# A sparse attention and gated feed-forward kernel: the order of its first loads

## The chip, the cores and the metric

The kernel runs on one core of a Trainium2 chip. The time is the device time of one execution in microseconds (us), and runs are compared by the median. A core has five engines with an instruction stream each: TensorE (PE, matmuls and transposes; PEld are its weight loads), VectorE (DVE), ScalarE (ACT), GpSimd (POOL) and SyncE (SP). Each engine takes its instructions strictly in the order of the program. Transfers are issued by SP, ACT and POOL and carried out by 16 DMA engines that all of them share.

## The reference

```python
# q, k, v: [4 batches, 8 heads, 768 tokens, 64], float32; sampled_blocks: [24, 3]
scores = (q @ k^T) / 8                       # per head, 768 x 768
mask: 24 x 24 blocks of 32 tokens; a block is kept if |i-j| <= 1, if i or j is 0 or 23,
      or if j is one of the three sampled blocks of row i
attn = softmax(where(mask, scores, -1e9)); x = attn @ v      # [4, 768, 512]
h    = relu(x @ w_in)                        # w_in [512, 1024]
conv = sum over k of conv_w[k] * h[token + k - 1]            # 3 taps along the tokens
out  = (h * sigmoid(conv)) @ w_out           # w_out [1024, 512], out [4, 768, 512] float32
```

## The kernel before, in words

**The attention.** The 32 heads are worked on as 16 pairs, P = 0 to 15, four pairs to a batch. A pair's q, k and v are two heads each. q and k of a pair come as bf16 into one of three `nat` buffers, v into one of three `vn` buffers; the load itself converts from float32. PE transposes q and k (`pe_head`, L482), and DVE copies the result out of PSUM (L488) into one of six slots, `ET` (even tokens of the regrouped order) and `OT` (odd ones). Rows 64 to 87 of a slot hold the mask: 24 further rows of the contraction that add a large negative number to the scores of blocks that are left out. The mask rows are the same for all slots. They are built in slot 0 and copied to slots 1 to 5: slot 1 by DVE (`rows_by`, L398, seen in the trace as L371), slots 2 to 5 by transfers that SP issues (`rows_to`, L392), two per slot.

The scores are worked off in 144 *units* of eight 128 x 128 blocks, 18 units to a half n of a batch (n = 0 to 7) and 4.5 units to a pair within it. A unit is: S, the score matmuls (L612) into one of two `st` buffers; the exponential on ACT (L619) of 128 x 1024 elements into one of five `pt` buffers; and AV, eight matmuls with `pt` as weights and v as the moving operand (L639), in two groups of four. v needs a DVE copy from `vn` to `VT` (L468) first. After a pair, DVE divides by the sums (L567, L568), and SP issues a transposing transfer (L589) that lays the pair's output into `xT`.

**The feed-forward.** For each half, when all four parts of `xT` have landed: eight times four matmuls with `winb` (L663), a relu on ACT or DVE (L674, L676), three taps of the convolution on DVE (L687, L693) with edge copies on POOL (L766, L767), the gate as a tanh on ACT (L703) with two DVE steps (L706, L715), then matmuls with `woutb` (L730), an eviction (L739, L741) and the store.

**The order of the work.** The order of each engine's instructions is not written by hand. A list scheduler (`Scheduler.run`) simulates all engines while the program is built. Every operation has durations for the engines that may take it, what it depends on, the buffers that it needs, a latency, an earliest time and a due time (`prio`). The planner repeatedly takes the operation that can start first on its engine and, among those that could start at the same time, the one with the earliest due time. The transfers are simulated as one more engine, `DQ`. The chip then runs each engine's list in that order, whatever the real durations are. `T(u)` is the planned time of unit u; `OFF` is how long after `T(18(n+1))` the feed-forward of half n is due; `S_FIRST`, `A_FIRST`, `R_FIRST` and `N_FIRST` move the due times of S, AV, the relus and the division; `XLAT` and `TLAT` are the planned latencies of the transposing transfers.

**The loads.** `swdge` (L432) issues a load from POOL; it has a `gate`, an operation that has to come first. `qk_loads` issues q and k of a pair, `v_load` its v. q0 and k0 are not among them: they come as float32 by SP and ACT and are converted by DVE or ACT into a `nat` buffer. The four weight loads (two halves of `winb`, two of `woutb`, 512 KB each in bf16, against 192 KB for a q, k or v) have due times 3.3, 3.4, 5.35 and 5.85 there, q of pair P has P, k has P + 0.1 (k1 has 0.6), v has P + 0.2 (v0 has 0.95). In the trace POOL issues in this order: q1, k1, v0, v1, q2, v2, k2, winb first half, q3, v3, k3, winb second half, woutb both halves, q4, k4 and so on.

Of the kernel before, what the change touches and what calls it, by code (L numbers as in the profile page):

```python
# [164 lines left out]
def kernel(  # L165
# [21 lines left out]
    NSLOT = 6  # L187
# [138 lines left out]
    def ind(base, sign, src):  # L326
# [64 lines left out]
    def rows_to(dst, src):  # L391
        return lambda e: nc.sync.dma_start(out=dst[64:88], in_=src[64:88])  # L392
# [4 lines left out]
    def rows_by(dst, src):  # L397
        return lambda e: copy_to(e, dst[64:88], src[64:88])  # L398
    e_mask = {0: op({"DVE": 0.38, "ACT": 0.72}, dup(ET[0]), T(1), [qm_e, km_e], earliest=T0 - 0.5)}
    o_mask = {0: op({"DVE": 0.38, "ACT": 0.72}, dup(OT[0]), T(1), [qm_o, km_o], earliest=T0 - 0.5)}  # L400
    for s in range(1, NSLOT):
        for t, m in ((ET, e_mask), (OT, o_mask)):
            if s == 1:
                m[s] = op({"DVE": 0.58}, rows_by(t[s], t[0]), T(4.5) - 1.5, [m[0]])
            else:
                m[s] = op({"SP": 0.46}, rows_to(t[s], t[0]), T(4.5 * s) - 6, [m[0]], lat=6.0)
    v_one = {}
    for s in range(NSLOT):
        v_one[s] = op({"DVE": 0.06}, lambda e, s=s: nc.vector.memset(VT[s][:, :, :, 64:65], 1.0), -5 + s)
# [22 lines left out]
    def swdge(dst, src, prio, dur, deps=(), early=0.0, alloc=None, uses=(), gate=i_sel,  # L432
              lat=None):
        i_ = op({"POOL": 0.8}, lambda e: nc.gpsimd.dma_start(out=dst(), in_=src), prio,
                list(deps) + [gate], lat=0.6, alloc=alloc, uses=uses, earliest=early)
        return i_, op({"DQ": dur}, None, prio, [i_], lat=lat, uses=(([alloc] if alloc else []) + list(uses)))

    win_ld, wout_ld = [], []
    for x in range(2):
        win_ld.append(swdge(lambda x=x: winb[:, :, 512 * x:512 * x + 512],  # L440
                            moe_w_in.rearrange("(fc p) ff -> p fc ff", p=128)[:, :, 512 * x:512 * x + 512],
                            3.3 + 0.1 * x, 3.0)[1])
        wout_ld.append(swdge(lambda x=x: woutb[:, 4 * x:4 * x + 4, :],
                             moe_w_out.rearrange("(ffc p) o -> p ffc o", p=128)[:, 4 * x:4 * x + 4, :],
                             5.35 + 0.5 * x, 3.0)[1])

    def qk_loads(P):
        b, h0 = P // 4, 2 * (P % 4)
        nb = Buf(P_nat)
        early, late = (T(load_u[P]), 6.0) if P > 3 else (0.0, None)  # L450
        iq, lq = swdge(lambda: dst_of(q, nat_t[nb.index][:, 0], True), src_of(q, b, slice(h0, h0 + 2)), P, 1.25,
                       early=early, alloc=nb, gate=bn1 if P == 1 else i_sel, lat=late)
        if P == 1:
            bn2.deps.append(iq)
        lk = swdge(lambda: nat_t[nb.index][:, 1], src_of(k, b, slice(h0, h0 + 2)), P + 0.1 if P > 1 else 0.6, 1.1, [iq],
                   early=early + (3 if P > 3 else 0), uses=[nb], gate=bn2 if P == 1 else i_sel, lat=late)[1]
        lk.deps.append(lq)
        return nb, lq, lk

    def v_load(P, deps):  # L460
        s = P % NSLOT
        vb = Buf(P_vn)
        b, h0 = P // 4, 2 * (P % 4)
        ld = swdge(lambda: vn_t[vb.index], src_of(v, b, slice(h0, h0 + 2)), P + 0.2 if P else 0.95, 1.1,
                   early=T(load_u[P]) + 6 if P > 3 else 0.0, alloc=vb, lat=6.0 if P > 3 else None)[1]

        def cp(e):
            nc.vector.tensor_copy(out=VT[s][:, :, :, 0:64],  # L468
                                  in_=vn_t[vb.index].rearrange("p h (c d) -> p h c d", c=6))
        return op({"DVE": 0.27}, cp, T(first_u[P]) - (1 if P == 0 else 6), [ld] + deps, uses=[vb, slot_b[P]])  # L470
# [28 lines left out]
    for P in range(NP):  # L499
        s = P % NSLOT  # L500
        if P < min(NPE, NSLOT):

            op({"DVE": 0.0}, None, -100 + P, alloc=slot_b[P])
        if P == 0:
            nb = Buf(P_nat)
            casts = []
            for hh in range(2):
                for x in range(2):
                    def cast(e, hh=hh, x=x, nb=nb):
                        copy_to(e, nat_t[nb.index][:, x, hh], stage0[2 * hh + x])  # L510
                    casts.append(op({"DVE": 0.28, "ACT": 0.4}, cast, -16 + 8 * hh, [hw[2 * hh + x]],
                                    alloc=nb if not casts else None, uses=[] if not casts else [nb]))
            for hh in range(2):
                ce, co = pe_head(0, hh, nb, casts[2 * hh:2 * hh + 2])
                qk_ready[(0, hh)] = [ce, co] + ([qm_e, qm_o, km_e, km_o] if hh == 0 else [e_mask[0], o_mask[0]])
        elif P < NPE:
            nb, lq, lk = qk_loads(P)
            for hh in range(2):
                ce, co = pe_head(P, hh, nb, [lq, lk] + ([slot_first[P]] if P >= NSLOT and hh else [])
                                 + ([slot_first[P - 1]] if P > NSLOT and not hh else []))  # L520
                qk_ready[(P, hh)] = [ce, co, e_mask[s], o_mask[s]]
        else:
            nb, lq, lk = qk_loads(P)
            due = T(first_u[P]) - 10
# [12 lines left out]
            ce = op({"DVE": 0.5}, put(ET, 0), due, [t0, t1, slot_first.get(P - 1)], alloc=slot_b[P], uses=[tb])  # L537
            co = op({"DVE": 0.5}, put(OT, 64), due, [ce], uses=[slot_b[P], tb])
            slot_first[P] = ce
            for hh in range(2):  # L540
                qk_ready[(P, hh)] = [ce, co, e_mask[s], o_mask[s]]
        v_ready[P] = v_load(P, [v_one[s]] + ([slot_first[P]] if P in slot_first else []))


    blk_order = [[(0, 0, 0), (0, 1, 2), (1, 0, 1)], [(1, 1, 0), (1, 2, 2), (0, 2, 1)]]
# [314 lines left out]
```

## Time and profile before

| | |
|---|---|
| runs shown | 229.33, 227.44, 228.6 us: median 228.6 |
| the profiled execution's own time | 229.36 us |
| its span, first to last instruction | 227.6 us |
| mean granted TensorE clock | 0.985 |
| busy in the span: PE, ACT, DVE, POOL | 90%, 84%, 81%, 34% |
| instructions | 6634 |
| DMA | 25.44 MB in all; 11.14 MB through POOL's queue, 13.49 MB through SP's |

Engine rows with a time and a duration are read as "start, duration, engine, line, operation, output <- input, count"; several instructions of a kind in a row are merged into one row. What stands in brackets is the idle time of the engine just before, and what ended it. A row of a table of stretches gives the stretch, its length, then for PE, PEld, DVE, ACT and POOL the busy time and in parentheses the number of instructions, then the granted clock of TensorE, the busy share of the DMA engines and their GB/s. Rows of waits read "who waited, line <- for whom: us in all, times, longest".

### The profile page before, as it was taken

The page shows a single profiled execution, that of the slowest core. Times are in us where ns is not written, and L with a number is a line of the kernel's source. Part 1 is how long each engine was busy: PE and PEld are TensorE (multiplying, and loading weights), DVE is VectorE, ACT ScalarE, POOL GpSimd, SP SyncE. Part 2 cuts the span into 40 slices and gives each one's busy share as a digit, 9 for nine tenths or more (in the row PEclk, how much of TensorE's full clock was granted, in tenths as well). Part 3 has the DMA queues.
Part 4 walks back from the last instruction along what each step waited for, and adds up shares of the span by engine and source line. Part 5 has one row for each costly group of instructions (what it writes and reads, how often), then busy time and mean ns, then how long its engine had stood idle before and what let it go on. Part 6 is the DMA issues. An engine that isn't in the chain of part 4 may idle for free. (4 is left out here: it accounts for less than half of the span.)

```text
span 227.6 us, 6634 instructions
## 1 busy us (share of the span) xinstructions
PE 204.7 (90%) x2592; PEld 153.6 (67%) x2610; DVE 185.3 (81%) x521; ACT 191.1 (84%) x248; POOL 77.8 (34%) x172
## 2 busy tenths in 40 slices
PE   7991699999998998998999999999999999899871
PEld 5881587788776775786778776887776778555330
DVE  5972331169999999999998999899999969999961
ACT  4883299999899989998999998999999999855441
POOL 8771420026364541352634451142132002146000
PEclk9999589999999999999999999999999999999999
DMA  7999999117989499698699856821200230111223
GB/s 170 150 216 205 205 193 167 30 21 93 114 107 122 54 134 208 132 170 115 95 174 138 177 108 145 123 61 57 68 20 20 66 109 20 63 49 46 92 92 138
DMA packets 48838, 25.44 MB, mean 112 GB/s; under 512 B 34768, under 2 KB 45544, under 8 KB 48808
## 3 DMA queue, kind: packets, MB, share of 16 engines
q0 software_dynamic: 18464, 11.14, 39.0%
q1 hardware_dynamic: 30056, 13.49, 26.3%
q8 instruction: 20, 0.33, 0.6%
q10 hardware_dynamic: 288, 0.39, 0.6%
q14 instruction: 10, 0.08, 0.1%
HBM read 23.08 MB, written 6.29 MB: 129 GB/s over the span
## 5 line engine op out<-in xcount | busy, mean ns | idle before, releaser
L619 ACT ACTIVATE pt<-st 128x1024 bf16<-128x1024 f32 x144 | 141.8, 1044 | 12.8 <-PE st L612 12.2
L639 PE MATMUL av<-vt,pt 128*128 128x65 bf16 x1152 | 59.3, 194 | 1.3 <-ACT pt L619 1.2
L687 DVE TENSOR_SCALAR m<-hE,cw 128x384 bf16<-128x384 bf16 x192 | 57.1, 346 | 1.7 <-POOL hE L772 0.7
L639 PEld LDWEIGHTS <-pt 128*128 128x128 bf16 x1152 | 51.0, 98 | 4.1 <-ACT pt L619 2.3
L663 PE MATMUL mix<-xT,winb 128*128 128x384 bf16 x240 | 47.2, 326 | 0.8 <-ACT hE L674 0.4
L766 POOL COPY hE<-hE 128x254 bf16<-128x254 bf16 x32 | 16.8, 524 | 80.0 <-ACT hE L674 38.0
L612 PE MATMUL st<-et,ot 88*128 88x128 bf16 (+1 forms) x224 | 43.0, 236 | 0.7 <-ACT pt L619 0.5
L612 PE MATMUL st<-ot 88*128 88x128 bf16 (+1 forms) x224 | 42.8, 235 | 0.4
L612 PE MATMUL st<-et 88*128 88x128 bf16 (+1 forms) x208 | 42.1, 243 | 0.4
L612 PE MATMUL st<-ot,et 88*128 88x128 bf16 (+1 forms) x208 | 41.6, 241 | 0.9 <-DVE ot L488 0.4
L730 PE MATMUL mix<-woutb,gT 128*128 128x512 bf16 x142 | 39.5, 379 | 3.2 <-DVE hE L676 1.3
L612 PEld LDWEIGHTS <-ot 88*128 88x128 bf16 x448 | 34.7, 98 | 11.1 <-issue 3.0
L612 PEld LDWEIGHTS <-et 88*128 88x128 bf16 x416 | 33.1, 98 | 10.1 <-issue 2.5
L693 DVE TENSOR_TENSOR m<-m 128x768 bf16<-128x768 bf16 x64 | 35.9, 565 | 0.5
L703 ACT ACTIVATE tn<-m 128x768 bf16<-128x768 bf16 x32 | 27.5, 858 | 6.1 <-DVE m L693 5.9
L663 PEld LDWEIGHTS <-winb 128*128 128x128 bf16 x256 | 22.3, 97 | 12.7 <-issue 1.1
L730 PEld LDWEIGHTS <-gT 128*128 128x128 bf16 x192 | 15.8, 97 | 19.0 <-DVE gT L715 3.5
L674 ACT ACTIVATE hE<-mix 128x384 bf16<-128x384 f32 x35 | 17.7, 515 | 2.7 <-PE mix L663 2.6
L568 DVE TENSOR_TENSOR xtok<-av,rcp 128x384 bf16<-128x384 f32 x32 | 17.8, 557 | 1.1
L676 DVE TENSOR_SCALAR hE<-mix 128x384 bf16<-128x384 f32 x25 | 13.8, 550 | 5.0 <-PE mix L663 5.0
L715 DVE TENSOR_TENSOR gT<-tn,hE 128x768 bf16<-128x768 bf16 x32 | 17.6, 549 | 0.1
L567 DVE RECIPROCAL rcp<-av 128x6 f32<-128x6 f32 x32 | 6.0, 189 | 14.0 <-PE av L639 13.9
(75 smaller groups left out, 183.9 us busy)
## 6 DMA issues: line engine op xcount, KB each, us to landing
out_dram<-o2s SPq DMA_DIRECT2D x24, 256.0 KB
vn<-in_v_dram POOLq DMA_DIRECT2D x16, 192.0 KB, 5.1
nat<-in_q_dram POOLq DMA_DIRECT2D x15, 192.0 KB, 4.5
nat<-in_k_dram POOLq DMA_DIRECT2D x15, 192.0 KB, 5.2
winb<-in_moe_w_in_dram POOLq DMA_DIRECT2D x2, 512.0 KB, 13.6
woutb<-in_moe_w_out_dram POOLq DMA_DIRECT2D x2, 512.0 KB, 16.6
xT<-xtok SPq DMA_TRANSPOSE x31
o2s<-in_k_dram ACTq DMA_DIRECT2D x2, 192.0 KB
```

Of the source, the lines that this page charges most:

```text
L568: nc.vector.tensor_tensor(out=xtok_t[xk.index].rearrange("p c h d -> p h c d"), in0=o[:, :, :, 0:64], in1=rcp.unsqueeze(3).broadcast_to([1 ...
L612: nc.tensor.matmul(out=st_t[stb.index][:, 128 * x:128 * (x + n_)], lhsT=QK[kc % 2][s][0:88, 1, hh, kc // 2, :], rhs=QK[par][s][0:88, 0, hh ...
L619: e_op = op({"ACT": t_act(1024)}, lambda e, stb=stb, ptb=ptb: nc.scalar.activation(out=pt_t[ptb.index], in_=st_t[stb.index], func=AF.Exp, ...
L639: nc.tensor.matmul(out=av_t[av_buf[(n, P % 4)].index][:, off:off + 65], lhsT=pt_t[ptb.index][:, 128 * x:128 * x + 128], rhs=VT[P % NSLOT][ ...
L663: nc.tensor.matmul(out=tiles[hb.index][:, 0:384], lhsT=winb[:, fc, 128 * ffc:128 * ffc + 128], rhs=xT_t[xt_buf[n].index][:, fc, :], start= ...
L674: nc.scalar.activation(out=dst, in_=src, func=AF.Relu, bias=0.0, scale=0.5)
L687: nc.vector.tensor_scalar(out=m_t[cb.index][:, slot, o0:o1], in0=src, scalar1=w, scalar2=None, op0=ALU.mult)
L693: nc.vector.tensor_tensor(out=m[:, 0], in0=m[:, 0], in1=m[:, 1], op=ALU.add)
L703: th = op({"ACT": 0.745}, lambda e: nc.scalar.activation(out=tn_t[cb.index], in_=m_t[cb.index][:, 0], func=AF.Tanh, bias=0.0, scale=0.5), ...
L715: nc.vector.tensor_tensor(out=o, in0=t, in1=h, op=ALU.mult)
L730: nc.tensor.matmul(out=acc(), lhsT=gT_t[gb.index][:, ffc, 128 * c:128 * c + 128], rhs=woutb[:, ffc, :], start=(ffc == 0), stop=(ffc == NFF ...
L766: nc.gpsimd.tensor_copy(out=h[:, f0:f0 + 2, 1:128], in_=h[:, f0:f0 + 2, 384:511])
```

## The change

The order of the loads is gated. k of every pair comes right behind its q, and v0 behind k1, v1 behind k2, v2 and v3 behind k3. The weights are issued behind v3. Pair 0's `nat` buffer is taken ahead of all others, so that q3 reuses the buffer of pair 0 and not that of pair 1. The identity matrix (`i_sel`) is made before k1 is issued. The mask rows of slot 2 are copied by DVE too, and the mask transfers of slots 4 and 5 get an earliest planned time of `T(26)` and `T(28)`. The planner's latency of a POOL load changes from 0.6 and 1.9 to 0 and 2.4 us, and the times and offsets for due times have other values.

```diff
-FLEX = 0.0
+FLEX = 0
...
-    T0, PACE0, PACE1 = 8.0, 0.966, 1.0
-    OFF = 14.635
-    XLAT, TLAT = 6.0, 7.0
-    S_FIRST, A_FIRST, R_FIRST, N_FIRST = 1.742, -0.618, 1.2, -0.122
-    F1S, F2A, F2S = 0.062, 1.8, 0.4
+    T0, PACE0, PACE1 = 8.0, 0.9, 1.018
+    OFF = 18.559
+    XLAT, TLAT = 6.652, 8.257
+    S_FIRST, A_FIRST, R_FIRST, N_FIRST = 4.551, -4, 0.593, 1.725
+    F1S, F2A, F2S = 0.03, 1.8, 0.4
...
     i_sel = op({"POOL": 0.3}, ...
-        pattern=[[-1, 128]], channel_multiplier=1), 0.9, [i_mem, bn2])
+        pattern=[[-1, 128]], channel_multiplier=1), -19.2, [i_mem, bn2])
...
-            if s == 1:
-                m[s] = op({"DVE": 0.58}, rows_by(t[s], t[0]), T(4.5) - 1.5, [m[0]])
+            if s < 3:
+                m[s] = op({"DVE": 0.58}, rows_by(t[s], t[0]), T(4.5 * s) - 2.5, [m[0]],
+                            earliest=T(4.5 * s - 4.5))
             else:
-                m[s] = op({"SP": 0.46}, rows_to(t[s], t[0]), T(4.5 * s) - 6, [m[0]], lat=6.0)
+                m[s] = op({"SP": 0.46}, rows_to(t[s], t[0]), T(4.5 * s) - 6, [m[0]], lat=6.0, earliest=T(18 + 2 * s) if s > 3 else 0.0)
...
     i_ = op({"POOL": 0.8}, lambda e: nc.gpsimd.dma_start(out=dst(), in_=src), prio,
-                list(deps) + [gate], lat=0.6, ...)
-        return i_, op({"DQ": dur}, None, prio, [i_], lat=lat, ...)
+                list(deps) + [gate], lat=0.0, ...)
+        return i_, op({"DQ": dur}, None, prio, [i_], lat=lat or 2.4, ...)
...
     (qk_loads)
-        lk = swdge(..., src_of(k, ...), P + 0.1 if P > 1 else 0.6, 1.1, [iq],
-                   early=early + (3 if P > 3 else 0), uses=[nb], gate=bn2 if P == 1 else i_sel, lat=late)[1]
-        lk.deps.append(lq)
+        ik, lk = swdge(..., src_of(k, ...), P + 0.1 if P > 1 else 0.6, 1.1, [iq],
+                   early=early + (3 if P > 3 else 0), uses=[nb], lat=late)
+        k_iss[P] = ik
...
     (v_load)
-        ld = swdge(..., src_of(v, ...), P + 0.2 if P else 0.95, 1.1, ...)[1]
+        v_iss[P], ld = swdge(..., src_of(v, ...), P + 1.15 if P < 3 else P + 0.2, 1.1, ...
+                              gate=k_iss[max(P, min(P + 1, 3))])
...
         if P == 0:
             nb = Buf(P_nat)
+            op({"POOL": 0.0}, None, -100, alloc=nb)
...
     (the weight loads, moved behind all v loads in the text of the program)
-   win_ld:  due 3.3 + 0.1 * x,  DQ 3.0        wout_ld: due 5.35 + 0.5 * x, DQ 3.0
+   win_ld:  due 3.3 + 0.1 * x,  DQ 2.7, gate=v_iss[3]
+   wout_ld: due 3.5 + 0.1 * x,  DQ 2.7, gate=v_iss[3]
```

More of the change, by code (lines that the diff above doesn't have):

```diff
@@ L434, in swdge @@
         i_ = op({"POOL": 0.8}, lambda e: nc.gpsimd.dma_start(out=dst(), in_=src), prio,
[L435 to L445, printed above, removed]
+                list(deps) + [gate], lat=0.0, alloc=alloc, uses=uses, earliest=early)
+        return i_, op({"DQ": dur}, None, prio, [i_], lat=lat or 2.4, uses=(([alloc] if alloc else []) + list(uses)))
+    win_ld, wout_ld, k_iss, v_iss = [], [], {}, {}
     def qk_loads(P):
@@ L541 @@
                 qk_ready[(P, hh)] = [ce, co, e_mask[s], o_mask[s]]
+    for P in range(NP):
+        s = P % NSLOT
         v_ready[P] = v_load(P, [v_one[s]] + ([slot_first[P]] if P in slot_first else []))
+    for x in range(2):
+        win_ld.append(swdge(lambda x=x: winb[:, :, 512 * x:512 * x + 512],
+                            moe_w_in.rearrange("(fc p) ff -> p fc ff", p=128)[:, :, 512 * x:512 * x + 512],
+                            3.3 + 0.1 * x, 2.7, gate=v_iss[3])[1])
+        wout_ld.append(swdge(lambda x=x: woutb[:, 4 * x:4 * x + 4, :],
+                             moe_w_out.rearrange("(ffc p) o -> p ffc o", p=128)[:, 4 * x:4 * x + 4, :],
+                             3.5 + 0.1 * x, 2.7, gate=v_iss[3])[1])
     blk_order = [[(0, 0, 0), (0, 1, 2), (1, 0, 1)], [(1, 1, 0), (1, 2, 2), (0, 2, 1)]]
```

8 lines of the change are left out of this document (4 added, 4 removed).

## The prediction

> **What bounds the kernel now.** I read the slices of the page first, to find out where the engines rest.
>
> ```profile
> PE   7991699999998998998999999999999999899871
> ACT  4883299999899989998999998999999999855441
> PEclk9999589999999999999999999999999999999999
> DMA  7999999117989499698699856821200230111223
> ```
>
> A slice is 5.7 us. From the sixth slice on PE and ACT are full up to the tail. The one hole is in the fourth and fifth slices (17 to 28 us): PE falls to 1, ACT to 3 and 2, the granted clock to 5, and the DMA engines are full. The table of stretches puts numbers to it.
>
> ```profile
> 20.00:30.00 10.00, 5.45 (x59) 4.90 (x60) 3.21 (x7) 2.48 (x3) 3.64 (x5) 0.66 1.27 202
> 30.00:45.00 15.00, 13.83 (x235) 11.90 (x233) 2.30 (x7) 14.86 (x17) 1.41 (x2) 1.00 0.92 127
> 60.00:195.20 135.20, 130.17 (x1764) 100.10 (x1777) 128.23 (x359) 130.35 (x168) 45.95 (x107) 1.00 0.65 104
> 195.20:227.60 32.40, 24.80 (x140) 11.74 (x138) 24.93 (x72) 16.02 (x28) 7.96 (x21) 1.00 0.21 82
> ```
>
> Between 60 and 195 us PE, DVE and ACT are busy for 130.2, 128.2 and 130.4 of 135.2 us. Three engines at 95 to 96% leave some 5 us each to be won, however the work is ordered. So the hole is the place. The chain of waits over the first 40 us, then the rows of PE, DVE and ACT around it:
>
> ```profile
> ACT pt L619 <- PE st L612: 9.9, 7, 7.5
> ```
> ```profile
> 14.80 0.34 PE L482 MATMUL mix<-ident,nat 128*128 128x128 bf16 x3 [0.40 <-DMA nat<-in_k_dram]
> 14.98 0.41 PE L639 MATMUL av<-vt,pt 128*128 128x65 bf16 x8
> ...
> 16.69 0.41 PE L639 MATMUL av<-vt,pt 128*128 128x65 bf16 x8
> ...
> 17.44 0.41 PE L639 MATMUL av<-vt,pt 128*128 128x65 bf16 x8
> 22.19 0.34 PE L482 MATMUL mix<-ident,nat 128*128 128x128 bf16 x3 [4.35 <-DMA nat<-in_q_dram]
> 24.89 0.50 PE L482 MATMUL mix<-ident,nat 128*128 128x128 bf16 x3 [2.36 <-DMA nat<-in_k_dram]
> 25.18 0.42 PE L612 MATMUL st<-et 88*128 88x256 bf16 x1
> ```
> ```profile
> 17.89 0.56 DVE L488 COPY ot<-mix 64x768 bf16<-64x768 bf16 x1
> ```
> ```profile
> 11.24 1.02 ACT L619 ACTIVATE pt<-st 128x1024 bf16<-128x1024 f32 x1 [0.27 <-PE st L612]
> 12.56 2.90 ACT L619 ACTIVATE pt<-st 128x1024 bf16<-128x1024 f32 x3 [0.30 <-PE st L612]
> 15.93 2.96 ACT L619 ACTIVATE pt<-st 128x1024 bf16<-128x1024 f32 x3 [0.47 <-PE st L612]
> 26.34 1.02 ACT L619 ACTIVATE pt<-st 128x1024 bf16<-128x1024 f32 x1 [7.46 <-PE st L612]
> 28.28 1.02 ACT L619 ACTIVATE pt<-st 128x1024 bf16<-128x1024 f32 x1 [0.91 <-PE st L612]
> 29.57 16.85 ACT L619 ACTIVATE pt<-st 128x1024 bf16<-128x1024 f32 x18 [0.27 <-PE st L612]
> ```
>
> Nine exponentials have run by 18.89 us: pairs 0 and 1 at 4.5 units each. Unit 9 needs only pair 2, whose last copy ends at 17.89 + 0.56 = 18.45 us. Yet its S runs at 25.18, because pair 3's transposes stand ahead of it in PE's order, and PE waits there for q3 until 22.19 and for k3 until 24.89. Pair 3's scores are not needed before unit 13. So the loss is one of order: the plan believed that q3 and k3 had landed. ACT, which paces the first 45 us (14.86 of 15 us after the hole), loses 7.46 + 0.91 + 0.27 = **8.64 us**.
>
> Why they are late is in POOL's list of issues:
>
> ```profile
> 7.54 0.72 POOL L434 DMA_DIRECT2D nat<-in_k_dram  x1
> 8.26 0.77 POOL L434 DMA_DIRECT2D winb<-in_moe_w_in_dram  x1
> 10.34 0.74 POOL L434 DMA_DIRECT2D nat<-in_q_dram  x1 [1.32 <-PE mix L482]
> 11.92 0.71 POOL L434 DMA_DIRECT2D vn<-in_v_dram  x1 [0.83 <-DVE vt L468]
> 12.63 0.72 POOL L434 DMA_DIRECT2D nat<-in_k_dram  x1
> ...
> 22.03 0.70 POOL L434 DMA_DIRECT2D nat<-in_k_dram  x1 [5.70 <-DMA winb<-in_moe_w_in_dram]
> ```
>
> The first row is k2, whose transposes could start at 14.80. Behind it stands the first half of winb, 512 KB; then q3 (issued at 10.34, landed by 22.19), v3 and k3 (issued at 12.63, landed by 24.89, 12.3 us later). k4, in the last row, waited for winb until 22.03. So winb landed just ahead of q3: POOL's queue delivers about in order of issue.
>
> **The change part by part.** *The loads.* Ahead of and with k3, POOL's queue carried ten loads of 192 KB and 512 KB of winb, 2432 KB. Now there are eight, q1, k1, v0, q2, k2, v1, q3, k3: 1536 KB. From the first issue at 2.01 us the 2432 KB took 22.9 us; at that rate 1536 KB take 14.4 us and k3 lands at **16.5 us**. That is ahead of 17.44 + 0.41 = 17.85, where PE came to the wait. The transfers that SP issues beside them are in that rate. Both ends: the issue of q3 no longer waits for pair 1's transposes (its 1.32 us), but for pair 0's, which end by 7.84:
>
> ```profile
> 7.34 0.50 PE L482 MATMUL mix<-ident,nat 128*128 128x128 bf16 x6
> ```
> ```profile
> nat<-in_k_dram POOLq DMA_DIRECT2D x15, 192.0 KB, 5.2
> ```
>
> So q3 goes out at about 7.9 and k3 at 8.6. With the median of 5.2 us from issue to landing it lands at 13.8, and with the 12.3 us that k3 itself took, at 20.9. I take 16.5, the rate over the same queue in the same stretch. At the late end the wait shrinks by only 24.89 - 20.9 = 4.0 us.
>
> *Where PE meets the wait.* The position is planned, and the plan now has k3 earlier. If pair 3's transposes come one unit earlier in PE's list, behind the AV row of 16.69, PE is there at 17.1, with k3 landed; three units earlier, behind the row of 14.98, at 15.4. Against 16.5 that is a wait of 0 to 1.1 us. I leave 0.75 us in the sum, nearer to the late end, since the plan has k3 by some 2 us before the 16.5 (eight loads at its 1.1 to 1.25 us each behind an issue at 2.8, and 2.4 us of latency: 14.6). Once PE doesn't rest, the two waits behind the hole have no cause: S matmuls of 256 columns took 0.42 us there against 0.27 elsewhere.
>
> ```profile
> 25.00:30.00 5.00, 5.00 (x56) 4.61 (x56) 3.21 (x7) 2.48 (x3) 1.48 (x2) 0.53 1.28 205
> ```
>
> The granted clock was 0.53 in that stretch, after PE had rested from 17.85 on but for two short groups. The Trainium skill ("TensorE: Matmul & The Clock Gate", "Part 1: The HAM clock gate") states that an idle window of about 3.4 us drops the array to half its clock and that a busy one restores it; the 0.53 agrees. Without that rule one might leave the 0.91 and 0.27 us standing, and the sum would be 1.18 us smaller.
>
> *What is late next.* Pair 2: k2 is the fifth load and not the seventh, so by the rate above it comes 384 KB, 3.6 us, earlier than 14.80; unit 9 isn't held by it. v2 is the ninth, behind k3: 1728 KB, 18.3 us. Its first use is AV of unit 9, after an exponential that can't start before 18.9, and so ends at 19.9. Cost nothing; at the late end (k3 at 20.9, one more load of 1.8 us) it is 2.8 us late, which five `pt` buffers, five exponentials of about 1 us, cover as far as S isn't queued behind that AV on PE. v3 is later still, but not used before unit 13.
>
> *The masks.* Eight transfers, two to a slot, were issued by SP; the first and the last row:
>
> ```profile
> 8.11 2.37 SPq L392 DMA_DIRECT2D et<-et  x2
> ...
> 14.40 0.71 SPq L392 DMA_DIRECT2D ot<-ot  x1
> ```
> ```profile
> 10.11 0.54 DVE L371 COPY ot<-ot 24x1536 bf16<-24x1536 bf16 x1
> 15.18 0.55 DVE L488 COPY et<-mix 64x768 bf16<-64x768 bf16 x1 [1.32 <-PE mix L482]
> ```
>
> Now two are left there, for slot 3; slot 2 costs DVE two more copies of 0.54, 1.1 us, as for slot 1 (the row at 10.11). They fit into DVE's hole of 1.32 us before 15.18; without that cover pair 2's copies come 1.1 us later. Slots 4 and 5 are needed from unit 36 on; their transfers stand on SP behind transposing transfers of `xT`, and units 11 to 28 alone fill the ACT row from 29.57 to 46.4 us. Nothing. POOL's first work that isn't a load comes late:
>
> ```profile
> 48.71 0.39 POOL L766 COPY hE<-hE 128x254 bf16<-128x254 bf16 x1 [15.14 <-ACT pt L619]
> ```
>
> So where v3's issue waits for v0's `vn` buffer, or a weight load for an older transfer, as k4 did, loads alone are held up. The Trainium skill ("SBUF — State Buffer", "SBUF: two separate sides") speaks against DVE copies beside POOL's loads: such a copy can lock GpSimd out of the port through which it writes descriptors. By it the two copies could hold up q3 or k3 by up to 1.1 us, landing at 17.6, and the sum would be about 1 us smaller. In the trace q3's issue at 10.34 began inside the copy of 10.11 to 10.65 and took 0.74 us, no longer than winb's 0.77.
>
> *The weights.* Behind v3 (1920 KB, 20 us) 2048 KB land by about 40 us at that rate. Their first user:
>
> ```profile
> L663 PE MATMUL mix<-xT,winb x240: 322/326/329, 45.1 to 208.0; 128*128 128x384 bf16 x120
> ```
> ```profile
> L619 ACT ACTIVATE pt<-st x144: 1005/1026/1193, 9.0 to 195.2; 128x1024 bf16<-128x1024 f32 x144
> ```
>
> (start of the first and of the last; the second row, the exponentials, is for the end of this text.) All of the first half shifted by 8 us gives 37 us for the first matmul with winb. Only winb's 1024 KB (2944 KB, 29.7 us) must be there; woutb's first matmul comes far later. Covered by 7 us.
>
> *The due times.* Feed-forward operations yield to attention for 18.559 - 14.635 = 3.9 us longer. Before, the plan had them due at T(18) + 14.6 = 40.0 us; the trace begins them at 45.1, which without the hole is 36.4. So they ran as soon as they were ready, ahead of their due time, and the rank did not hold them. Between 30 and 45 us DVE works 2.3 us of 15: nothing else would take their place. I take zero. From both sides: 3.9 us lost if their start now follows the due time, and up to 3.7 us gained, half of the 7.5 us for which DVE rests in the last 32.4 us, if later feed-forward work fills the tail.
>
> **The sum.** 8.64 - 0.75 = 7.9 us, masks 0, weights 0, due times 0. The profiled execution took 229.36 us, its span 227.6; it becomes 221.5 with a span of 219.7. The median of the runs, 228.6, is 0.8 below that execution, so I forecast **220.7 us**.
>
> **The rivals.**
>
> *Half given back* (0.15). The hole goes, but the feed-forward of the first half starts at its later due time and runs 3.9 us behind to the end: 220.7 + 3.9 = 224.6. For it: three full engines from 60 us on can't catch up. Against it: the 36.4 above.
>
> *The queue is slow for another reason* (0.10). k3 takes its 12.3 us from whatever issue, lands at 20.9, and 4.0 us are won: 224.6 too. For it: other loads with 5.2 us as median share the same 16 engines. Against it: winb's landing just ahead of q3's.
>
> *It doesn't do what it says* (0.08). The planner, with other costs, puts another load's consumer in front of a unit that needn't wait for it, such as AV of unit 9 waiting for v2 or pair 4's transposes behind the weights, and the hole reappears elsewhere: within 1%, 226.3 to 230.9.
>
> *Slower* (0.07). The feed-forward of half 0 starts later than 45.1 us. It was due at 40.0 and began 5.0 later; due at 8 + 18 x 0.9 + 18.559 = 42.8 now, with the same lag, it begins at 47.8. Everything from 60 us on is full, so the end moves by the 2.7 us: 231.3. The point from which it decides is 45.1 us for the first matmul with winb. Against it: readiness, not the due time, set that start, and readiness comes with the attention.
>
> **How the numbers follow.** My forecast has 0.60: 217 to 223.5 us. Low end of the range: the three short waits of ACT before the hole go too (0.27, 0.30 and 0.47 us, 9.7 in all, 218.9), and 2.4 us of DVE's rest in the tail: 216.5. High end: the rivals at 224.6 with one more load of 1.8 us waited for: 226.4, taken as 226.5. What is left out is the last two rivals and a little of each tail. Within 1% is about what a measurement of this kernel can tell from no change; faster by more holds 0.60 + 0.15 + 0.10 = 0.85, no change 0.08, slower 0.07.
>
> **What would show it.** Right: no wait of PE for `nat` over 1 us before 30 us; k3's transposes before 18 us; the tenth exponential at about 19 us; granted clock 1.00 throughout 20 to 30 us; the first matmul with winb at 36 to 38 us; the last exponential at about 187 and not 195 us, with a tail of 32 us behind it. Wrong: a new wait of PE for `vn` or `nat`, a first matmul with winb after 41 us, or a tail longer than 35 us.

## The result and the profile after

The changed kernel takes **220.21 us** (median of four runs, 220.18 to 220.26) against 228.31 us (227.44 to 229.33) for the kernel before: a ratio of 0.9644, interval 0.9602 to 0.9686. The forecast was 220.7 us. The profiled execution took 220.20 us, with a span of 218.4 us and a mean granted clock of 1.0. Two executions in this document, one of the kernel before (413.99 us) and one of old_loads_same_plan (343.06 us), ran in a slower state and are left out of all medians, ranges and ratios.

The slices of the page of the changed kernel, 5.46 us each:

```profile
PE   7999999998989979999999899998999999899781
ACT  5499999999999989999999999999899999665531
PEclk9999999999999999999999999999999999999999
DMA  6999999999765996992999878221310040111214
```

The hole is gone: from the third slice on neither PE nor ACT falls below 7 until the tail, and the granted clock is 90% or more in every slice. The table of stretches of the changed kernel (columns as before):

```profile
20.00:30.00 10.00, 9.22 (x157) 7.91 (x156) 3.83 (x9) 10.00 (x12) 2.17 (x3) 1.00 1.29 184
30.00:45.00 15.00, 14.46 (x246) 12.64 (x244) 7.65 (x19) 14.84 (x18) 4.06 (x8) 1.00 1.53 170
184.30:218.40 34.10, 26.27 (x146) 12.73 (x145) 27.25 (x81) 17.48 (x31) 9.55 (x25) 1.00 0.20 77
```

ACT is busy for all of the 10 us in which it had been busy for 2.48. The third row is the tail, from the start of the last exponential: 34.10 us against 32.40. Then the waits of the first 40 us, and the rows of PE and of ACT around the place where the hole was:

```profile
ACT pt L624 <- PE st L617: 1.5, 2, 1.2
```
```profile
16.77 0.41 PE L644 MATMUL av<-vt,pt 128*128 128x65 bf16 x8
17.47 0.49 PE L476 MATMUL mix<-ident,nat 128*128 128x128 bf16 x6 [0.29 <-DVE ot L482]
```
```profile
10.41 7.75 ACT L624 ACTIVATE pt<-st 128x1024 bf16<-128x1024 f32 x8 [1.19 <-PE st L617]
18.51 20.65 ACT L624 ACTIVATE pt<-st 128x1024 bf16<-128x1024 f32 x22 [0.35 <-PE st L617]
```

ACT waits for S twice, 1.5 us in all, where it had waited 9.9 us. The 1.19 are before the first exponential. Pair 3's transposes (17.47, six for one head's q and k) follow an AV with no wait for `nat`: the 0.29 us are for a DVE copy out of PSUM. k3 had landed by then. POOL's row of its issue, and the row of the transfers issued at that moment, with the time from issue to landing at the end:

```profile
9.03 0.72 POOL L435 DMA_DIRECT2D nat<-in_k_dram  x1
```
```profile
nat<-in_k_dram POOLq DMA_DIRECT2D x1, 192.0 KB, 7.5
```

9.03 + 7.5 = 16.5 us.

**How far the attention moved.** The second ACT row holds units 8 to 29, one every 0.935 us, so unit 28 begins at 18.51 + 20 x 0.935 = 37.2 us. Before, the row at 29.57 held units 11 to 28, and the last of them began at 29.57 + 16.85 - 1.02 = 45.4. That is **8.2 us earlier**; the rest of the program behind it got 1.0 us shorter (227.6 - 45.4 = 182.2, now 218.4 - 37.2 = 181.2). Together these are the 9.2 us of the two spans. The rows by line of the changed kernel (first and last start):

```profile
L668 PE MATMUL mix<-xT,winb x240: 322/326/329, 38.2 to 196.1; 128*128 128x384 bf16 x120
```
```profile
L624 ACT ACTIVATE pt<-st x144: 1005/1025/1132, 10.4 to 184.3; 128x1024 bf16<-128x1024 f32 x144
```

Counted from the first matmul with `winb` the same 9.2 us are 6.9 (45.1 to 38.2) and 2.3: the feed-forward now starts about a unit later against the attention.

### The profile page after: what moved, and what is told of

The parts are those of the page before. It is cut to its first block, busy times and chain, and to the rows that moved or that the text cites. A ratio compares the mean times of both kernels' runs of the same rounds, so it can differ in the third digit from the quotient of the medians.

```text
span 218.4 us, 6627 instructions
## 1 busy us (share of the span) xinstructions
PE 201.8 (92%) x2593; PEld 151.8 (69%) x2610; DVE 185.7 (85%) x525; ACT 190.5 (87%) x246; POOL 77.9 (36%) x172
## 3 DMA queue, kind: packets, MB, share of 16 engines
q0 software_dynamic: 18464, 11.14, 43.7%
## 4 chain that ended last, share of the span: by engine, by line
DVE 53%; PE 30%; ACT 10%; issue 4%; DMA 1%; ACTq 0%; DVEq 0%
DVE m L692 17%; DVE m L698 11%; PE st L617 10%; ACT pt L624 8%; PE mix L668 6%; PE av L644 5%; PE mix L735 5%; DVE gT L720 5%; DVE xtok L573 4%; DVE hE L681 3%; DVE tn L711 3%; PE av L318 2%; DVE ot L371 2%; DVE et L482 2%; DVE et L371 2%
## 5 line engine op out<-in xcount | busy, mean ns | idle before, releaser
L692 DVE TENSOR_SCALAR m<-hE,cw 128x384 bf16<-128x384 bf16 x192 | 55.6, 340 | 1.9 <-ACT hE L679 0.9
L644 PE MATMUL av<-vt,pt 128*128 128x65 bf16 x1152 | 56.9, 193 | 0.0
L644 PEld LDWEIGHTS <-pt 128*128 128x128 bf16 x1152 | 49.5, 97 | 3.1 <-ACT pt L624 0.4
L617 PE MATMUL st<-ot,et 88*128 88x128 bf16 (+1 forms) x208 | 40.7, 239 | 1.4 <-DVE ot L371 0.6
L617 PE MATMUL st<-et 88*128 88x128 bf16 (+1 forms) x208 | 41.2, 239 | 0.3
L771 POOL COPY hE<-hE 128x254 bf16<-128x254 bf16 x32 | 16.1, 503 | 65.3 <-DVE hE L681 36.6
L617 PEld LDWEIGHTS <-et 88*128 88x128 bf16 x416 | 32.1, 97 | 9.6 <-issue 3.3
L435 POOL DMA_DIRECT2D vn<-in_v_dram x16 | 11.4, 716 | 21.2 <-DVE vt L462 18.5
L435 POOL DMA_DIRECT2D nat<-in_q_dram x15 | 11.8, 785 | 10.4 <-PE mix L476 5.3
```

The costliest lines, as they stand in the source:

```text
L617: nc.tensor.matmul(out=st_t[stb.index][:, 128 * x:128 * (x + n_)], lhsT=QK[kc % 2][s][0:88, 1, hh, kc // 2, :], rhs=QK[par][s][0:88, 0, hh ...
L644: nc.tensor.matmul(out=av_t[av_buf[(n, P % 4)].index][:, off:off + 65], lhsT=pt_t[ptb.index][:, 128 * x:128 * x + 128], rhs=VT[P % NSLOT][ ...
L692: nc.vector.tensor_scalar(out=m_t[cb.index][:, slot, o0:o1], in0=src, scalar1=w, scalar2=None, op0=ALU.mult)
```

## The experiments

Each run's time is a median with its lowest and highest; the ratio is to the kernel before on the same chip (its median there lay between 228.1 and 228.7 us). S1 is the start of the first matmul with `winb` in the profiled execution, and "rest" the span less S1. All kernels are cut from the kernel before or from the changed one. A planned program has fixed instruction lists for each engine. Where an edit changes what the planner is told, the lists can change in places that have nothing to do with the edit; so some experiments keep the lists of the changed kernel and alter only what an instruction in them does.

| run | time, us | ratio and interval | S1 | span | rest |
|---|---|---|---|---|---|
| before | 228.31 (227.44 to 229.33) | 1 | 45.1 | 227.6 | 182.5 |
| changed | 220.21 (220.18 to 220.26) | 0.9644 (0.9602 to 0.9686) | 38.2 | 218.4 | 180.2 |
| weights_late_only | 225.8 (223.83 to 227.18) | 0.9873 (0.9797 to 0.9948) | 39.0 | 222.1 | 183.1 |
| nat_first_only | 226.94 (225.63 to 227.95) | 0.993 (0.9899 to 0.9961) | 43.7 | 226.3 | 182.6 |
| new_due_times_only | 228.49 (227.78 to 229.81) | 1.0017 (0.9986 to 1.0048) | 44.9 | 226.7 | 181.8 |
| winb_ahead_unplanned | 222.9 (220.99 to 223.43) | 0.9724 (0.9662 to 0.9787) | 41.9 | 221.6 | 179.7 |
| winb_ahead_planned | 219.81 (219.79 to 220.13) | 0.962 (0.9584 to 0.9656) | 38.2 | 218.3 | 180.1 |
| old_loads_same_plan | 224.49 (223.84 to 225.67) | 0.9841 (0.9756 to 0.9925) | 44.2 | 223.8 | 179.6 |
| masks_by_transfer_same_plan | 223.98 (222.71 to 225.0) | 0.9808 (0.9734 to 0.9882) | 41.1 | 220.6 | 179.5 |
| start_same_plan | 218.87 (218.64 to 219.28) | 0.9586 (0.9511 to 0.9662) | 37.1 | 217.2 | 180.1 |
| old_due_times | 226.63 (226.32 to 226.93) | 0.9919 (0.9887 to 0.9951) | 36.9 | 225.2 | 188.3 |
| same_loads_off_18_4 | 224.68 (224.25 to 225.43) | 0.9845 (0.9778 to 0.9912) | 37.4 | 222.7 | 185.3 |
| old_off_only | 240.19 (238.97 to 242.2) | 1.0543 (1.046 to 1.0626) | 38.2 | 238.7 | 200.5 |
| earlier_start | 228.12 (227.79 to 229.25) | 1.0011 (0.999 to 1.0032) | 38.3 | 227.1 | 188.8 |

### The weights alone

The kernel before, with the four weight loads moved behind the v loads and gated. The lists of PE, DVE and ACT stay those of before.

```diff
-   win_ld:  due 3.3 + 0.1 * x         wout_ld: due 5.35 + 0.5 * x
+   win_ld:  ..., gate=v_iss[3]        wout_ld: ..., gate=v_iss[3]
```

> The kernel before with one thing of the change: the four weight loads are issued behind v3 (due times, masks, v order and buffers as before). Theory (the hole is made by 512 KB of winb ahead of q3 and k3): q3 still waits for pair 1's buffer until about 10.3 us and k3 goes out at about 12.6; it is the tenth load of 192 KB, so by 106 KB/us it lands at 20.1 us, at the least 17.8 (5.2 us behind its issue). PE comes to pair 3's transposes at 17.9, so the hole shrinks from 8.6 to 0 to 2.5 us: 221 to 223. Rival (the new due times carry the gain): 227 to 229. Rival (the queue was slow for other reasons): k3 at 24 us or later, 227 to 229.

225.8 us, 2.8 us above the slow end of what was expected, and scattered over 3.4 us; the profiled execution was the fastest of its four. Its rows of PE and of ACT:

```profile
15.76 0.34 PE L475 MATMUL mix<-ident,nat 128*128 128x128 bf16 x3 [1.45 <-DMA nat<-in_k_dram]
...
20.69 0.34 PE L475 MATMUL mix<-ident,nat 128*128 128x128 bf16 x3 [1.71 <-DMA nat<-in_k_dram]
```
```profile
16.89 2.96 ACT L620 ACTIVATE pt<-st 128x1024 bf16<-128x1024 f32 x3 [1.52 <-PE st L613]
21.57 16.71 ACT L620 ACTIVATE pt<-st 128x1024 bf16<-128x1024 f32 x18 [1.72 <-PE st L613]
```

k3 comes at 20.69 and not at 24.89, so the half of `winb` was part of the delay. But PE still waits for k2 (1.45 us) and k3 (1.71 us), since v1 and v2 stand ahead of k2, and the mask transfers run beside all of them. The gate is a good part of the change, not all of it.

### Pair 0's buffer alone, and the due times alone

```diff
 nat_first_only (in the kernel before):
+            op({"POOL": 0.0}, None, -100, alloc=nb)
 new_due_times_only (in the kernel before): the ten constants of the diff (PACE0 to F1S), OFF = 18.559 among them
```

> The kernel before with one line of the change: pair 0 takes its nat buffer first, so that q3 takes over pair 0's. On POOL q3 then stands ahead of winb's first half, but k3 still behind it. Theory (bytes in front of k3): 9 x 192 + 512 = 2240 KB, by 106 KB/us k3 lands at 23.1 us, and the hole shrinks by 1.8 us: 226 to 227.5. Rival (q3's wait for a buffer, 1.3 us, made the hole): 220 to 224.

> The kernel before with the planner's times and offsets of the change (T0 to F2S) and nothing else. The hole stays, since loads and buffers are as before and pair 3's transposes keep their place behind the S of nine units. Theory (the old due times cost 6 us only in the order that the new loads make; in the kernel before the middle was already full): 226 to 230. Rival (the new due times pack the middle better whatever the loads): 221 to 225.

The buffer alone is worth 1.4 us (the new plan also moves one of the first conversions from DVE to ACT); the due times make no difference that the runs can tell (1.0017, interval 0.9986 to 1.0048). PE of the first, ACT of the second:

```profile
17.93 0.33 PE L482 MATMUL mix<-ident,nat 128*128 128x128 bf16 x3
23.71 0.50 PE L482 MATMUL mix<-ident,nat 128*128 128x128 bf16 x3 [5.45 <-DMA nat<-in_k_dram]
```
```profile
24.60 1.02 ACT L619 ACTIVATE pt<-st 128x1024 bf16<-128x1024 f32 x1 [5.85 <-PE st L612]
```

With the buffer, q3 is there in time and k3 is still 5.45 us late: half of `winb` stands ahead of it (v3 is now issued behind it). With the new due times alone the hole stays.

### The place of the wait, apart from the loads

In the changed kernel, half of `winb` is issued ahead of q3 again. In one version the planner's model of the queue still delivers it behind k3, by due time (3.3); in the other, in the order of issue (2.2). Nothing else in the program differs. The first keeps the lists of PE, DVE and ACT of the changed kernel; in the second PE and DVE have pair 3's transposes and copies at another place.

```diff
-   3.3 + 0.1 * x, 2.7, gate=v_iss[3])
+   3.3 + 0.1 * x if x else 2.2, 2.7, gate=v_iss[3 if x else 1], dqp=None if x else 3.3)   # unplanned
+   3.3 + 0.1 * x if x else 2.2, 2.7, gate=v_iss[3 if x else 1], dqp=None if x else 2.2)   # planned
```

> The changed kernel with the first half of winb issued ahead of q3, and the planner still believing that this transfer runs behind q3 and k3 (its due time in the planner's queue is 3.3). Pair 3's transposes keep their place on PE, behind the S of eight units. Theory (bytes ahead of k3 in POOL's queue, met by a place in PE's order that doesn't know it): k3 lands 2.6 to 4.8 us later than its 17.0, PE stands still for 2.1 to 4.3 us from 17.5 on, and the time is 222.5 to 225. Rival (due times, masks and buffers made the gain; winb doesn't matter): 220 to 221.

> The same order of issue as in the run with winb ahead of q3, one number other: the planner's queue has winb in front too (2.2 and not 3.3). Now pair 3's transposes stand behind the S of eleven units on PE. Theory (the loss is the planner's mistake about the place, since pair 3 isn't needed before unit 13): k3 is as late as in that run, but units 8 to 10 run meanwhile; PE comes to the transposes at about 20.5 us and waits 0 to 1.5 us: 220.2 to 222. Rival (k3 itself is needed then, so lateness alone costs): as that run, 222.5 to 225.

222.9 against 219.81 us, the second 0.4 us below what was expected. PE and ACT of the unplanned version:

```profile
17.90 0.34 PE L476 MATMUL mix<-ident,nat 128*128 128x128 bf16 x3 [1.22 <-DMA nat<-in_q_dram]
18.93 0.50 PE L476 MATMUL mix<-ident,nat 128*128 128x128 bf16 x3 [0.69 <-DMA nat<-in_k_dram]
```
```profile
20.38 1.02 ACT L624 ACTIVATE pt<-st 128x1024 bf16<-128x1024 f32 x1 [2.71 <-PE st L617]
```

and of the planned one:

```profile
19.86 0.83 PE L476 MATMUL mix<-ident,nat 128*128 128x128 bf16 x12
```
```profile
14.53 21.48 ACT L624 ACTIVATE pt<-st 128x1024 bf16<-128x1024 f32 x23 [0.30 <-PE st L617]
```

Both issue the same loads in the same order. The unplanned one has pair 3's transposes behind 8 units in PE's list and waits; the planned one has them behind 11, where the loads have landed, and ACT runs through. This shows the mechanism of the hole of before: there too the planner's queue serves q3, k3 and v3 (due 3.0 to 3.2) ahead of `winb` (3.3), while POOL had issued `winb` first. The unplanned version also tells what half of `winb` ahead of q3 costs with the lists of the change: 222.9 - 220.2 = 2.7 us. `winb` ahead of q3 costs nothing where the plan knows of it (219.79 to 220.13 against 220.18 to 220.26).

### The old order of loads, and the masks, with the changed lists

The lists are those of the changed kernel. In the first kernel, the first 14 load issues in POOL's list carry the loads in the order of before. In the second, slot 2 is filled by SP's transfers instead of DVE's copies, and those of slots 4 and 5 go out with slot 3's, as before the change.

```diff
 old_loads_same_plan
+        for o, x in zip(ld, [0, 1, 2, 5, 3, 8, 4, 10, 6, 9, 7, 11, 12, 13]):
+            o.fn = fns[x]
 masks_by_transfer_same_plan
-   m[s] = op({"DVE": 0.58}, rows_by(t[s], t[0]), ...
+   m[s] = op({"DVE": 0.58}, rows_by(t[s], t[0]) if s == 1 else rows_to(t[s], t[0]), ...
+   more = [rows_to(t[x], t[0]) for x in range(3, NSLOT)] if s == 3 else []
```

> The changed kernel, its plan untouched: every engine's list is the same, only the first POOL issues carry other loads, in the order of the kernel before (q1, k1, v0, v1, q2, v2, k2, winb first half, q3, v3, k3, winb second half, woutb). So the loads' order is tried without a new order of anything else. Theory (the load order is the gain): k3 has 896 KB more in front of it and lands 4.6 (at 194 KB/us) to 8.4 us (at 106) after its 17.0, PE stands still from 17.5 to 21.6 to 25.4, and the time is 224.3 to 228. Rival (the rest of the change makes the gain): 220 to 221.5.

> The changed kernel, its plan untouched, with the mask rows as before the change: slot 2 by two transfers instead of two copies on VectorE, and the transfers of slots 4 and 5 issued at once behind those of slot 3. Theory (the transfers share the engines with the loads): 432 KB more between 9 and 15 us, k3 lands 2 to 4 us later than 17.0, 221.5 to 224. Rival (the masks hardly weigh): 219.7 to 221.

The order of the loads alone is worth 224.5 - 220.2 = 4.3 us, the masks alone 3.8 us, both at the median; the runs of the two spread over 1.8 and 2.3 us. PE with the old order of loads, where k2 is waited for as well as q3 and k3:

```profile
15.57 0.34 PE L476 MATMUL mix<-ident,nat 128*128 128x128 bf16 x3 [1.20 <-DMA nat<-in_k_dram]
...
19.13 0.34 PE L476 MATMUL mix<-ident,nat 128*128 128x128 bf16 x3 [0.58 <-DMA nat<-in_q_dram]
21.12 0.50 PE L476 MATMUL mix<-ident,nat 128*128 128x128 bf16 x3 [1.65 <-DMA nat<-in_k_dram]
```

PE and POOL with the masks by transfers:

```profile
19.02 0.34 PE L477 MATMUL mix<-ident,nat 128*128 128x128 bf16 x3 [2.28 <-DMA nat<-in_k_dram]
```
```profile
8.41 0.72 POOL L436 DMA_DIRECT2D nat<-in_k_dram  x1
```

Six mask transfers more, 432 KB, beside the loads, and k3 lands 19.02 - 8.41 = 10.6 us after its issue. In old_off_only (below), whose first loads and mask copies are those of the change, PE also waits for k3 and so shows its landing. POOL and PE of that kernel:

```profile
8.36 0.73 POOL L435 DMA_DIRECT2D nat<-in_k_dram  x1
```
```profile
17.63 0.34 PE L476 MATMUL mix<-ident,nat 128*128 128x128 bf16 x3 [0.52 <-DMA nat<-in_k_dram]
```

17.63 - 8.36 = 9.3 us there. With the masks by transfers k3 lands 1.4 us later than in old_off_only and 2.5 us later than in the change (16.5); the time is 3.8 us longer at the median.

### The due times in the changed kernel

```diff
 old_due_times:        the same ten constants, as in the kernel before
 old_off_only:         OFF = 18.559  ->  OFF = 14.635
 same_loads_off_18_4:  OFF = 18.559  ->  OFF = 18.4
```

> The changed kernel with the planner's times and offsets of before (T0 to F2S); loads, gates, masks and buffers of the change. Theory (ranks decide little, since feed-forward work starts as soon as it is ready): within 1% of the changed kernel, 219 to 222.5. Rival (later due times of the feed-forward, earlier S and later AV carry part of the gain): 223 to 226.

> The changed kernel with one number of before: the feed-forward due 14.635 us behind its half and not 18.559. With all old times it lost 6.4 us, between 65 and 105 us, where PE waited for the gates and VectorE for output matmuls. Theory (feed-forward work that is due too early stands in front of attention and then waits there in order): most of the loss comes back, 223 to 227. Rival (the offsets of S, AV, relu and division, or the pace, make it): 219.5 to 221.5.

> The changed kernel with the feed-forward due 18.4 us behind its half and not 18.559. Loads and the order of all engines up to about 40 us are the same; after that the lists differ in many places. Theory (the runs with other due times lost their 6 to 20 us because any new order of the middle makes the engines wait for each other, not because of where the due times stand): between 221 and 228, with the attention as early as in the changed kernel. Rival (an earlier due time costs in proportion: 3.9 us of OFF cost 20 us): 0.16 us earlier costs 0.8 us, 220.5 to 221.3.

The first two expectations were missed on the slow side, by 4 and by 13 us (226.63 and 240.19). The third run was to tell whether the time follows OFF in proportion, which would have given 220.5 to 221.3 us; at 224.68 it does not. The starts of all three are no later than that of the change (S1 36.9, 38.2 and 37.4); what grew is the rest. A stretch of 20 us in the middle, first of the changed kernel, then of the one with OFF at 18.4:

```profile
85.00:105.00 20.00, 19.90 (x276) 15.25 (x275) 19.61 (x55) 19.78 (x26) 8.71 (x22) 1.00 0.91 128
```
```profile
85.00:105.00 20.00, 18.62 (x253) 14.21 (x251) 16.45 (x45) 19.02 (x25) 8.14 (x19) 1.00 0.75 112
```

DVE loses 3.2 us there, and the other engines some too. The engines wait for each other there; the waits of DVE in old_off_only over 2 us, from 90 to 150 us:

```profile
96.92 0.56 DVE L681 TENSOR_SCALAR hE<-mix 128x384 bf16<-128x384 f32 x1 [2.56 <-PE mix L668]
...
147.63 0.56 DVE L681 TENSOR_SCALAR hE<-mix 128x384 bf16<-128x384 f32 x1 [3.02 <-PE mix L668]
```

So 0.16 us of one due time, with the same loads and an attention as early, cost 4.5 us.

### The start

The changed kernel starts its exponentials at 10.41 us and the kernel before at 9.03. One experiment replanned the start; the other kept the lists of winb_ahead_planned, issued `winb` behind v3, left out four of the warm-up matmuls, and exchanged two copies of pair 0, so that each head's `et` is followed by its `ot`.

```diff
 earlier_start (replanned)
-   co = op(..., [t, ce], ...)                        +   co = op(..., [t] if P == 0 else [t, ce], ...)
-   last = op({"PE": 0.22 if x < 15 else 0.11}, ...   +   last = op({"PE": 0.22 if x < 24 else 0.11}, ...
 start_same_plan (lists kept)
+   (warm-up matmuls)  fn = (lambda e: None) if 18 <= x < 22 else ...
+    c0[1].fn, c0[2].fn = c0[2].fn, c0[1].fn
+    for o, x in zip(ld, [0, 1, 2, 3, 4, 5, 7, 8, 9, 10, 6, 11, 12, 13]):  o.fn = fns[x]
```

> The changed kernel with two edits that aim at its first exponential, which begins at 10.4 us against 9.0 before: the copies of pair 0 go et, ot, et, ot on VectorE (the odd copy no longer depends on the even one), and the planner counts 24 and not 15 warm-up matmuls at 0.22 us, which is what they take. Theory (the start is on the path): first exponential at 9.0 to 9.5, 218.8 to 219.8. Rival (k3, which lands at about 17.0, is then what PE waits for, and eats it): 220 to 221.

> A try to beat both kernels without a new order of the middle: the plan of the run with winb ahead and planned (pair 3's transposes behind the S of eleven units), winb issued behind v3 as in the changed kernel, four of the 23 warm-up matmuls ahead of the mask's matmuls left out (0.22 us each), and VectorE's copies for pair 0 in the order et, ot, et, ot. Theory (the first exponential, at 10.4 us, is on the path): it begins at 9.0 to 9.6 and the time is 218.6 to 219.3. Rival (the feed-forward's own waits set the end): 219.7 to 220.3.

The replanned one lost all that the change had won (228.12 us where 218.8 to 219.8 were expected), though it starts earlier (first exponential at 9.15, S1 38.3): its rest is 188.8 us. The one with the lists kept is the fastest kernel of this study, **218.87 us**, 218.64 to 219.28 in its four runs. Its ACT and PE:

```profile
8.99 2.92 ACT L627 ACTIVATE pt<-st 128x1024 bf16<-128x1024 f32 x3 [0.91 <-PE st L620]
12.12 1.02 ACT L627 ACTIVATE pt<-st 128x1024 bf16<-128x1024 f32 x1 [0.21 <-PE st L620]
13.46 24.61 ACT L627 ACTIVATE pt<-st 128x1024 bf16<-128x1024 f32 x26 [0.32 <-PE st L620]
```
```profile
18.79 0.83 PE L476 MATMUL mix<-ident,nat 128*128 128x128 bf16 x12
```

Its exponentials begin 1.4 us before those of the change, and unit 28 1.1 us before (13.46 + 24 x 0.944 = 36.1). old_off_only shows what an earlier start meets where pair 3's transposes stand behind 8 units: its first exponential is at 9.70 us, 0.7 before that of the change, and PE then waits for k3 until 17.63, so that ACT goes on at 18.51 in both.

## Why the prediction was right, step by step

**What bounded the kernel: right, and shown.** The hole came from the place of pair 3's transposes in PE's list against a late k3. Moving the place alone (unplanned against planned) is worth 3.1 us; moving the landing alone, with the place kept, 2.7 us (half of `winb`), 4.3 us (all loads) and 3.8 us (masks).

**The 8.64 - 0.75 = 7.9 us: right in sum, in part by luck.** Unit 28 came 8.2 us earlier. In place of the 8.64 us of waits stands one of 0.35. Two terms that the sum left out nearly cancel: the three short waits of before (0.27 + 0.30 + 0.47 = 1.04 us) are gone too, and the first exponential came 1.38 us later. 8.64 - 0.35 + 1.04 - 1.38 = 7.95; the other 0.2 us are spread over the exponentials. The late start was not priced at all. The lists have a part in it: 23 warm-up matmuls now stand ahead of the mask matmuls where 20 stood, and pair 0's copies come `et`, `et`, `ot`, `ot`. But with the same lists the first exponential came at 9.44 us in winb_ahead_unplanned, so up to 1.0 of the 1.38 us is scatter (last section).

**From the profiled execution to the median: luck.** It was to become 221.5 us and became 220.20: 0.3 us more from the attention and 1.0 from the rest. The 0.8 us taken off for the median then made up for most of that. The median of the changed kernel, 220.21, is no lower than its profiled execution.

**k3 at 16.5 us: right, but the rate behind it was not.** It landed at 16.5. The rate of 106 KB/us, over the whole queue with the transfers of SP in it, had two errors of opposite sign. It charged too much for bytes: the 896 KB more that old_loads_same_plan puts ahead of k3 would cost 8.4 us by it, and k3 came at 21.1, 4.6 us later than in the change; half of `winb` would cost 4.8, and put back ahead of q3 it moved k3 to 18.9, by 2.4. And it charged nothing for the mask transfers, with which k3 came at 19.0, 2.5 us later. These shifts are rough, since with the same loads in the same order k3 landed at 16.5 in the change, at 16.1 in earlier_start and at 17.6 in old_off_only. The two also act on each other. Half of `winb`, in the kernel before and in the unplanned version:

```profile
winb<-in_moe_w_in_dram POOLq DMA_DIRECT2D x1, 512.0 KB, 13.2
```
```profile
winb<-in_moe_w_in_dram POOLq DMA_DIRECT2D x1, 512.0 KB, 9.7
```

Issued at 8.26, it landed at 21.5 before, 6.7 us behind the load ahead of it (k2, 14.8), with eight mask transfers beside it. Issued at 7.53 in the unplanned version, it landed at 17.2, 3.6 us behind the load ahead of it (v1, 13.6), with two. In the other runs with this half ahead of k3 the same interval is 2.7 and 4.0 us with two mask transfers (old_loads_same_plan, winb_ahead_planned) and 5.5 and 5.7 us with eight (nat_first_only, new_due_times_only). So `winb` ahead of k3 and the masks beside it made k3 late together.

**PE one unit earlier: right.** The transposes stand behind 8 units and not 9, and PE came to them at 16.77 + 0.41 = 17.18, with k3 landed since 16.5. In the sum, 0.75 us had been kept for a wait, and in this profile there was none for k3; in old_off_only it was 0.52. The plan has k3 at 13.3 + 2.4 = 15.7 us and not at the 14.6 of the prediction, since the four float32 loads of q0 and k0 stand first in the planner's queue.

**The clock: the two waits behind the hole are gone, and a short rest is enough to bring them back.** The granted clock stayed at 1.00, and 0.91 and 0.27 us went with the hole, as forecast. But PE rested only 1.22 + 0.69 us for q3 and k3 in the unplanned version and 2.28 us for k3 with the masks by transfers, less than the idle window of 3.4 us that the prediction quotes, and the granted clock fell to 0.50 and 0.57 behind that. The stretches, unplanned first:

```profile
19.00:25.00 6.00, 6.00 (x65) 5.51 (x65) 3.38 (x8) 3.17 (x4) 3.09 (x5) 0.50 1.25 203
```
```profile
19.00:23.00 4.00, 3.98 (x44) 3.56 (x45) 2.06 (x5) 2.05 (x2) 2.34 (x3) 0.57 1.23 201
```

ACT then waits 0.27, 0.91 and 0.27 us more in the first and 0.31 and 0.64 in the second. So a late k3 costs more than PE's wait for it.

**Masks at nothing: wrong.** The prediction asked only whether the moved transfers have users in time and what the DVE copies cost. It did not ask what the transfers took from the loads beside them. With the lists kept they are worth 3.8 us. The old order of loads and the old masks together, 4.3 + 3.8 = 8.1, happen to be the whole gain; nothing shows that the two add up. weights_late_only and nat_first_only, 2.9 and 1.4 us against the kernel before on the same chip, have only a part of the change each, and k3 is still late.

**The DVE copies.** By the Trainium skill ("SBUF — State Buffer", "SBUF: two separate sides") they could lock GpSimd out. POOL's issues beside them kept their length, as the rows of POOL and of DVE in the changed kernel show:

```profile
12.75 1.51 POOL L435 DMA_DIRECT2D winb<-in_moe_w_in_dram  x2
14.23 1.51 POOL L435 DMA_DIRECT2D woutb<-in_moe_w_out_dram  x2
```
```profile
13.87 0.78 DVE L371 COPY et<-et 24x1536 bf16<-24x1536 bf16 x1
...
14.89 0.55 DVE L371 COPY ot<-ot 24x1536 bf16<-24x1536 bf16 x1
```

Two issues took 1.51 us, 0.76 each, and the first copy took 0.78 us in place of 0.55. So POOL did not lose. The copy, which began inside an issue, took 0.2 us more; no run shows why. The sum without the rule stands.

**Weights at nothing: right.** The first matmul with `winb` began at 38.2 us, 0.2 us past its forecast of 36 to 38. PE's waits between 30 and 60 us in the changed kernel have one row:

```profile
PE mix L476 <- DVE ot L482: 0.6, 1, 0.6
```

It is not for a weight load.

**Due times at nothing, bounds of -3.7 and +3.9: wrong as a bound.** In the kernel before they are worth nothing that the runs can tell. In the changed one the same constants are worth 6.4 us, and one of them alone 20. The step that failed is the picture that a due time shifts the feed-forward and nothing else. It draws another order of the whole middle, and there the engines can lose more to each other than the due time moves. With the change's lists, kept or nearly so, the rest behind S1 stays at 179.5 to 180.2 us whatever the first 40 us do (six kernels); the lists of before give 182.5 to 183.1 (182.5, 183.1 and 182.6); replanned ones 181.8 to 200.5. So the rest of the change's lists is 1 to 2.3 us shorter than before, by one marker or the other, by an order that happened to be good, and that the prediction did not see: luck, as far as the forecast goes.

**The ends.** The last exponential came at 184.3 and not at 187, the tail at 34.1 and not at 32: attention ran 2.7 us ahead of its forecast, and the tail gave 2.1 back.

**The rivals.** *Slower* needed a first matmul with `winb` after 45.1 us; it began at 38.2, ahead even of its due time of 42.8. *Half given back* needed it 3.9 us behind the 36.4 of the prediction, at 40.3. It began 1.8 us behind, and the shorter rest took that back. *The queue is slow for another reason* was partly so: the masks were another reason. But it was taken away with the rest. *It doesn't do what it says* is refuted by the rows at 17.47 and 18.51.

**What stays open.** Why the rest of one order is 180 us and that of another 185 to 200 was followed only to the waits shown. It was not traced to single choices of the planner. How the 8.2 us divide among gate, order of v, buffer and masks has no one answer, since they all act on the same k3. Why k3 lands up to 1.5 us apart with the same loads, and why `winb` is so much slower beside the mask transfers, was not followed further.

## What to carry to other kernels

Where a planner serves a queue by due time and the hardware serves it about in the order of issue, the plan puts a consumer in front of its data, and an in-order engine stops for it. Look for a wait whose consumer is not needed yet, and price a move of loads by what runs beside them too. Test the parts of a planned kernel with the instruction lists kept; a replanned comparison mixes the edit with a new order of everything, and 0.16 us of a due time moved this kernel by 4.5 us.

## What was not expected of the hardware

The same first 23 warm-up matmuls, from the same start, took 5.09 us in the changed kernel and 4.38 us in the one with OFF at 18.4:

```profile
1.29 5.09 PE L318 MATMUL av<-warm 128*128 128x256 bf16 x23 [1.29 <-DVE warm L312]
```
```profile
1.29 4.38 PE L318 MATMUL av<-warm 128*128 128x256 bf16 x23 [1.29 <-DVE warm L312]
```

The start of a kernel thus moves by 0.7 us with no change to its first instructions. And the time from issue to landing of a load is not set by its bytes: k3, always 192 KB, took 7.5 us in the changed kernel, 9.3 in old_off_only with the same loads ahead of it, 10.6 with the masks by transfers, 12.3 before, and 21.12 - 12.73 = 8.4 us in old_loads_same_plan, where it was issued 3.7 us later and waited behind other loads for less time:

```profile
12.73 0.72 POOL L435 DMA_DIRECT2D nat<-in_k_dram  x1
```
